# A second level of seven-product multiplication for part of a dense layer, computed among the first sequence products

## The chip, the cores and the metric

The kernel runs on one core of a Trainium2 chip. The metric is the device time of one execution in microseconds (us). About 0.2% of it, 1.7 us, is what a measurement of this kernel can tell from no change.

## The reference

The input is `x` with 2048 tokens of 640 channels. Two branches are computed and mixed by a gate per token.

```python
g = sigmoid((x * gate_w).sum(-1, keepdims=True))
# branch A: Fourier mixing, real part
a = x @ dft_hid_re.T;  b = x @ dft_hid_im.T
A = dft_seq_re @ a - dft_seq_im @ b
# branch B: dense 640 -> 1728, mish, dense 1728 -> 640
h = x @ w1 + b1
B = (h * tanh(softplus(h))) @ w2
return g * A + (1 - g) * B
```

## The kernel before

**Products.** Everything is float32. An operand is kept as a pair of tiles, `h` (rounded to the matmul's format) and `l` (the rest). ACT makes the first (`operand` L328, `split` L319), DVE the second by a subtraction (L329, L320). One block product of 128x128 weights with 128x512 moving data is three matmuls, h·h, h·l and l·h (`mm3`, all on line 334). So every operand that is made costs one row on ACT and one on DVE.

**Seven instead of eight.** Each large product is cut in 2x2 blocks and made by a scheme of seven block products instead of eight, at the price of sums and differences of blocks on DVE (`tt`, L298) and of partial results that are copied out of an accumulator bank and added later. There are eight such banks, `ps0` to `ps7`, of 128x512.

**Stages.** In program order: the sequence products of `x` with the two Fourier matrices (four `Problem`s `sq[0..3]`, each with the phases `first`, `second`, `third`; the results go to DRAM as `u`); the hidden products (`hd`, results `y`); the dense layer with `w1` and mish (`dense_rest`, `dense_first`, results `act`); the last product with `w2` (`ou`), which also adds `y` and writes the output. `gates` computes the gate of every token during the sequence stage.

The first phases of `sq[0]`, `sq[1]` and `sq[2]` open the kernel. In a first phase eight tiles of a Fourier matrix are loaded, made operands and multiplied with three blocks of `x` each: nine matmuls for one new operand.

**The dense layer before.** The outputs are 13 full groups `f` of 128 columns and one of 64. Groups 12 and 13 (`dense_rest`) are made plainly for each of the four token blocks `t` of 512. Groups 0 to 11 are made by `dense_first(tp)`: token blocks 2tp and 2tp+1 are the two rows of blocks, channels 0-255 and 256-511 the two columns, groups `f` and `f+6` the two halves of the weights; channels 512-639 are a plain fifth part (`d1`, `d2`). For each `f` that makes 18 block products: a11 2, s1 2, d2 1, s2 2, s4 2, d1 1, s3 2, a12 2, d1 1, a22 2, d2 1. Two groups `f` go side by side and use all eight banks.

**What sets the order.** The code records each instruction in a `Graph`. PE's order is the order of the code. All other instructions get a due time (`want`, computed backwards from the matmuls that need them in `wants`), and `run` walks through a model of the five engines, hands out buffers (18 tiles `f`, 6 tiles `x`, 10 operand pairs `r`, 26 weight pairs `w`) and writes each engine's instructions in the order in which the model starts them. On the chip each engine then executes its own list strictly in that order. ACT, DVE and the DMA queues therefore run the lists that the model chose, and a row that waits holds up all rows behind it on its engine. SP issues the loads, POOL issues most stores.

Of the kernel before, what the change touches and what calls it, by code (L numbers as in the profile page):

```python
# [47 lines left out]
class Graph:  # L48
# [71 lines left out]

    def run(self, pools):
# [103 lines left out]
def fnet_mish_gate(ctx: ExitStack, tc: tile.TileContext, xn, xt, c_re, c_im, wd_re, wd_im,  # L225
                   w1a, w1b, b1a, b1b, w2, gw, out):
    nc = tc.nc
# [370 lines left out]
    def raw(t, k):  # L598
        return load(FS, xt[t, k])
# [8 lines left out]
    def w1_block(f):  # L608
        if f in W1:
            return  # L610
        ga, gb, t = load(X, w1a[f], cols=D), load(X, w1a[f + FP], cols=D), Val(X)
        a, b, c = W1[f] = Val(W), Val(W), Val(W)
        if f // KD not in T2B:
            T2B[f // KD] = Val(W)
        split(a, 0, ga, 0, D)
        split(b, 2, gb, 2 * P, 3 * P)
        tt(ga, gb, ga, OP.subtract, (A2, A2, A2), n=2 * P)
        tt(t, gb, ga, OP.subtract, (A2, B2, A2), n=2 * P)
# [3 lines left out]
        split(c, 4, t, 0, P)  # L622
        split(T2B[f // KD], f % KD, t, P, P)
        split(b, 0, t, 2 * P, 2 * P)
        split(c, 2, gb, 0, 2 * P)

    def w1_rest():
        if W1C:
            return
        W1C.append(Val(W))  # L630
        split(W1C[0], 0, load(X, w1a[FC - 1], cols=D), 0, D)
# [46 lines left out]

    def dense_first(tp, ready):
        t1, t2 = 2 * tp, 2 * tp + 1  # L680
        x = dict(ready)

        def get(name, make):
            if name not in x:
                x[name] = operand(make(), W if name[0][0] == "a" else R)
            return x[name]

        def sums_of(k):
            if k in summed:
                return  # L690
            summed.add(k)
            a21, a22, a11, a12 = raw(t2, k), raw(t2, k + 2), raw(t1, k), raw(t1, k + 2)
# [4 lines left out]
            raws.update({("s1", k): s1, ("s2", k): a22, ("s3", k): a21, ("s4", k): a12})  # L697
        raws, summed = {}, set()

        def op(name, k=0):  # L700
            if name[0] == "s":
                if (name, k) not in x:
                    sums_of(0)
                    sums_of(1)
                return get((name, k), lambda: raws.pop((name, k)))
            t, kk = {"a11": (t1, 0), "a12": (t1, 2), "a22": (t2, 2), "d1": (t1, 4), "d2": (t2, 4)}[name]
            return get((name, k), lambda: raw(t, kk + k))

        def times(b, name, blocks, start, stop):
            for k, w in enumerate(blocks):  # L710
                mm3(b, w, op(name, k), start and k == 0, stop and k == len(blocks) - 1)

        for f0 in range(0, FP, 2):
            pair_ = (f0, f0 + 1)
            for f in pair_:
                w1_block(f)
            w = {f: W1[f] for f in pair_}
            bk = {f: [bank() for _ in range(4)] for f in pair_}
            p1, p5, u2 = {}, {}, {}
            for f in pair_:  # L720
                times(bk[f][0], "a11", [(w[f][0], k) for k in range(2)], True, True)
                p1[f] = to_sbuf(bk[f][0])
            for f in pair_:
                times(bk[f][1], "s1", [(w[f][2], k) for k in range(2)], True, True)
                p5[f] = to_sbuf(bk[f][1])
            for f in pair_:
                times(bk[f][3], "d2", [(w[f][1], 4)], True, True)
            for f in pair_:
                times(bk[f][0], "s2", [(w[f][2], 4), (T2B[f // KD], f % KD)], False, True)
                u2[f] = to_sbuf(bk[f][0])  # L730
            for f in pair_:
                times(bk[f][1], "s4", [(w[f][1], 2 + k) for k in range(2)], False, False)
                times(bk[f][1], "d1", [(w[f][1], 4)], False, True)
# [5 lines left out]
            for f in pair_:  # L739
# [23 lines left out]

    nc.scalar.preload_act_table_set("sigmoid_and_others")
    ones = nc.const_aps.tensor(1.0, [P, N], mybir.dt.bfloat16)
# [17 lines left out]
    def gates():  # L783
# [8 lines left out]
        cols = [(gcol, k) for k in range(KS)]  # L792
        act(lambda: nc.scalar.activation(gcol.t, gcol.t, AF.Sigmoid), cols, cols, KS)
        dve(lambda: nc.vector.tensor_scalar(qcol.t, gcol.t, -1.0, 1.0, op0=OP.mult, op1=OP.add), cols, whole(qcol), KS)
# [8 lines left out]
    def c_tile(m):  # L803
        return lambda t, k: load(FS, (c_re, c_im)[m][t, k], by=HEAD.get(("c", k), 1e9) if not (m or t) and G.pe < 5 else 1e9)

# [10 lines left out]

    sq = [Problem(seq, q // 2, c_tile(q % 2), put_u(q % 2), aside=aside(f"ps{q}") if q in (1, 2) else None) for q in range(4)]
    hd = [Problem(hid, tp, lambda t, k: load_of(FS, usc[k][t]), put_y, aside=aside("ph") if tp else None,
# [4 lines left out]

    sq[0].first(seq_top)
    sq[1].first(seq_top)
    sq[2].first(seq_top)
    for c, src in ((b1s.t[:, :FC], b1a), (b1s.t[:FR, FC:], b1b)):
        dma("SP", lambda c=c, src=src: nc.sync.dma_start(c, src), [], whole(b1s), P * FC * 4)
    for q in range(4):
        if q == 3:  # L830
            sq[3].first(seq_top)
        sq[q].second(seq.low)
# [5 lines left out]
    for p in hd:  # L838
        p.second(hid.low)
        p.third()  # L840
    for t in (2, 3):
        dense_rest(t, [operand(raw(t, k)) for k in range(KD)])
    have = {}
    for t, names in ((0, ("a11", "a11", "a12", "a12", "d1")), (1, ("a21", "a21", "a22", "a22", "d2"))):
        xs = [operand(raw(t, k), W if n in ("a11", "a12", "a22") else R) for k, n in enumerate(names)]
        for k, n in enumerate(names):
            if n != "a21":
                have[n, k % 2 if k < 4 else 0] = xs[k]
        dense_rest(t, xs)
    dense_first(0, have)  # L850
    dense_first(1, {})
    ou[0].first(fin.top)
# [50 lines left out]
```

## Time and profile before

| | |
|---|---|
| median of three runs | 865.41 us (865.31 to 866.7) |
| the profiled execution's own time | 865.36 us |
| its span, first to last instruction | 863.6 us (1.8 us lie around it) |
| PE busy | 858.6 us, 99% |
| DVE busy | 672.0 us, 78% |
| ACT busy | 460.6 us, 53% |
| moved by DMA | 202.05 MB, mean 234 GB/s |

Nearly the whole span is the chain of matmuls on PE; the other engines have time left over the whole span, but DVE hardly has any in the first 140 us. A busy share over the whole span therefore says little about one stage.

### The profile page before, as it was taken

The page shows a single profiled execution, that of the slowest core. Times are in us where ns is not written, and L with a number is a line of the kernel's source. Part 1 is how long each engine was busy: PE and PEld are TensorE (multiplying, and loading weights), DVE is VectorE, ACT ScalarE, POOL GpSimd, SP SyncE. Part 2 cuts the span into 40 slices and gives each one's busy share as a digit, 9 for nine tenths or more (in the row PEclk, how much of TensorE's full clock was granted, in tenths as well). Part 3 has the DMA queues.
Part 4 walks back from the last instruction along what each step waited for, and adds up shares of the span by engine and source line. Part 5 has one row for each costly group of instructions (what it writes and reads, how often), then busy time and mean ns, then how long its engine had stood idle before and what let it go on. Part 6 is the DMA issues. An engine that isn't in the chain of part 4 may idle for free.

```text
span 863.6 us, 11923 instructions
## 1 busy us (share of the span) xinstructions
PE 858.6 (99%) x3772; PEld 708.0 (82%) x3772; DVE 672.0 (78%) x1183; ACT 460.6 (53%) x829; POOL 78.3 (9%) x142
## 2 busy tenths in 40 slices
PE   9999999999999999999999999999999999999998
PEld 6888888888888888888888888888888888888886
DVE  7999997876786577998878999915677899758493
ACT  7765536544553544777454657745655765533242
POOL 0000002001100200002002002111122100004000
PEclk9999999999999999999999999999999999999999
DMA  9986969764955474759864959455353778638943
GB/s 335 334 275 240 344 227 363 265 214 135 363 170 208 164 256 145 267 184 335 283 198 152 360 196 357 152 188 196 136 172 144 268 287 301 205 117 174 359 167 121
DMA packets 102175, 202.05 MB, mean 234 GB/s; under 512 B 12768, under 2 KB 15584, under 8 KB 102112
## 3 DMA queue, kind: packets, MB, share of 16 engines
q1 hardware_dynamic: 90416, 165.51, 55.8%
q0 software_dynamic: 11552, 35.66, 11.9%
q8 instruction: 29, 0.48, 0.2%
q14 instruction: 34, 0.28, 0.1%
q10 hardware_dynamic: 144, 0.13, 0.0%
HBM read 162.96 MB, written 38.29 MB: 233 GB/s over the span
## 4 chain that ended last, share of the span: by engine, by line
PE 99%; DMA 0%; ACT 0%; DVE 0%; issue 0%; ACTq 0%
PE ps L334 99%; DMA f<-in_xn_dram 0%; ACT f L307 0%; DVE w0l L320 0%; ACT w0h L319 0%; DVE x L580 0%; ACT x L578 0%; DVE r0h L326 0%; ACTq L578 0%; ACTq L307 0%
## 5 line engine op out<-in xcount | busy, mean ns | idle before, releaser
L298 DVE TENSOR_TENSOR f<-f,f 128x512 f32<-128x512 f32 x308 | 207.2, 686 | 14.6 <-DMA f<-in_c_im_dram 5.2
L298 DVE TENSOR_TENSOR f<-ps,f 128x512 f32<-128x512 f32 x99 | 64.8, 685 | 45.7 <-PE ps L334 45.5
L307 ACT ACTIVATE f<-ps 128x512 f32<-128x512 f32 x132 | 76.8, 594 | 38.1 <-PE ps L334 30.3
L290 POOL DMA_DIRECT2D u<-f x40 | 21.5, 540 | 320.7 <-DVE f L298 308.1
L603 ACT ACTIVATE f<-f,b1s 128x512 f32<-128x512 f32 x36 | 25.6, 722 | 29.5 <-DVE f L298 29.3
L290 POOL DMA_DIRECT2D act<-f x52 | 28.2, 542 | 134.7 <-DVE f L298 72.9
L328 ACT ACTIVATE r1h<-f 128x512 fp32r<-128x512 f32 x39 | 24.6, 630 | 28.0 <-PE ps L334 17.8
L328 ACT ACTIVATE r8h<-f 128x512 fp32r<-128x512 f32 x39 | 24.5, 629 | 27.9 <-PE ps L334 17.0
L328 ACT ACTIVATE r2h<-f 128x512 fp32r<-128x512 f32 x38 | 23.9, 630 | 27.1 <-PE ps L334 22.8
L328 ACT ACTIVATE r4h<-f 128x512 fp32r<-128x512 f32 x39 | 24.5, 629 | 25.0 <-PE ps L334 20.7
L328 ACT ACTIVATE r0h<-f 128x512 fp32r<-128x512 f32 x37 | 23.3, 630 | 27.2 <-PE ps L334 16.9
L329 DVE TENSOR_TENSOR r1l<-f,r1h 128x512 fp32r<-128x512 f32 x39 | 26.9, 688 | 12.5 <-ACT r1h L328 12.5
L328 ACT ACTIVATE r6h<-f 128x512 fp32r<-128x512 f32 x38 | 23.9, 628 | 20.9 <-PE ps L334 12.3
L329 DVE TENSOR_TENSOR r5l<-f,r5h 128x512 fp32r<-128x512 f32 x38 | 26.1, 688 | 11.0 <-ACT r5h L328 11.0
L298 DVE TENSOR_TENSOR x<-x,x 128x256 f32<-128x256 f32 (+1 forms) x77 | 32.0, 426 | 3.4 <-DMA x<-in_w_dram 2.0
L329 DVE TENSOR_TENSOR r2l<-f,r2h 128x512 fp32r<-128x512 f32 x38 | 26.1, 688 | 10.8 <-ACT r2h L328 10.8
L328 ACT ACTIVATE r7h<-f 128x512 fp32r<-128x512 f32 x38 | 23.8, 627 | 19.7 <-PE ps L334 16.1
L328 ACT ACTIVATE r3h<-f 128x512 fp32r<-128x512 f32 x38 | 23.9, 629 | 19.3 <-PE ps L334 11.4
L328 ACT ACTIVATE r9h<-f 128x512 fp32r<-128x512 f32 x37 | 23.3, 629 | 19.9 <-PE ps L334 14.2
L329 DVE TENSOR_TENSOR r0l<-f,r0h 128x512 fp32r<-128x512 f32 x38 | 26.2, 689 | 9.5 <-ACT r0h L328 9.2
L328 ACT ACTIVATE r5h<-f 128x512 fp32r<-128x512 f32 x38 | 23.9, 628 | 17.9 <-PE ps L334 15.7
L329 DVE TENSOR_TENSOR r7l<-f,r7h 128x512 fp32r<-128x512 f32 x38 | 26.1, 688 | 9.3 <-ACT r7h L328 9.1
(2005 smaller groups left out, 2661.1 us busy)
## 6 DMA issues: line engine op xcount, KB each, us to landing
f<-in_c_re_dram SPq DMA_DIRECT2D x128, 256.0 KB, 4.6
f<-in_c_im_dram SPq DMA_DIRECT2D x128, 256.0 KB, 4.3
f<-act SPq DMA_DIRECT2D x81, 256.0 KB, 5.1
f<-u SPq DMA_DIRECT2D x80, 256.0 KB, 5.3
act<-f POOLq DMA_DIRECT2D x52, 256.0 KB, 3.0
f<-in_xt_dram SPq DMA_DIRECT2D x44, 256.0 KB, 5.0
u<-f POOLq DMA_DIRECT2D x40, 256.0 KB, 5.5
x<-in_xn_dram SPq DMA_DIRECT2D x24, 320.0 KB, 4.5
```

Source lines behind the costliest of these rows:

```text
L290: dma(queue, lambda: ISSUE[queue].dma_start(d.t, v.t[:rows]), whole(v), whole(d), rows * N * 4)
L298: dve(lambda: nc.vector.tensor_tensor(o.t[rows, x], a.t[rows, y], b.t[rows, z], op=op), whole(a, b), whole(o), n)
L307: act(lambda: nc.scalar.activation(o.t, a.t, AF.Copy, scale=scale), whole(a), whole(o))
L328: act(lambda: nc.scalar.activation(r.t[0][:, :N], src.t[:, :N], AF.Copy), whole(src), [(r, 0)])
L329: dve(lambda: nc.vector.tensor_tensor(r.t[1][:, :N], src.t[:, :N], f32(r.t[0][:, :N]), op=OP.subtract), whole(src) + [(r, 0)], [(r, 1)])
L334: G.add("PE", lambda: nc.tensor.matmul(bank.t, w.t[wn][:, k * P:k * P + P], x.t[xn_][:, :N], start, stop, skip_group_check=True), [(w, (k, ...
L603: act(lambda: nc.scalar.activation(o.t[rows], src.t[rows], AF.Mish, **more), whole(src, table) + whole(b1s) * bias, whole(o), more=0.1)
```

## The change

For token blocks 0 and 1, two of the seven products (a11 with b11, and a12 with b21 together with its fifth part) have to be made for all six `f`. In the changed kernel the pairing of token blocks is (0,2) and (1,3), so that these two products of both pairs, taken over token blocks 0 and 1, over two channel blocks of 128 and over `f` 0-2 against 3-5, are again 2x2 block products. They are made by a second level of seven, in two pieces:

- `early_first` (channels 0-255): 7 block products for each of three units `j`, results stored to DRAM as `early`.
- `early_second` (channels 256-511 and the fifth part): 7 + 4 block products for each unit, added to `early`, then bias, mish and the store to `act`.
- `early_rests`: groups 12 and 13 of token blocks 0 and 1, which were made in the dense stage before.

These pieces stand between the first phases: `sq[1].first`, `early_first`, `sq[2].first`, `early_second`, `sq[3].first`, `early_rests`, `sq[0].first`; then the second and third phases follow. The three units of a piece take turns, one block product (or two) each. `dense_first` now makes 13 block products for each `f`: a11, a12 and one d1 are gone, and the first partial result is loaded from `early`. It uses six banks instead of eight.

Counted over the program, the dense layer has 730 matmuls in place of 748. SP and POOL issue 37 and 15 transfers more, ACT has 66 and DVE 58 instructions more. The mish table is loaded at the start, the sigmoid table for the gates, and the mish table again: three table loads in place of two. `wants` has a new last pass, which moves an instruction's due time behind those of what it needs.

```diff
+        for op in self.ops:
+            if op.engine != "PE":
+                op.want = max([op.want] + [(d.at if d.engine == "PE" else d.want) + d.took for d in op.deps])
...
+    def w1_twice(k0, fifth=False):
+        C, w, at, n, tiles = slice(0, H * P), {}, {}, 0, []
+        for i in range(2):
+            for j in range(2):
+                w[f"b{i + 1}{j + 1}"] = load(FS, w1h[k0 + i, j], cols=H * P)
+        for o, x, y in (("t1", "b12", "b11"), ("t2", "b22", "t1"), ("t3", "b22", "b12"), ("t4", "b21", "t2")):
+            w[o] = Val(FS)
+            tt(w[o], w[x], w[y], OP.subtract, (C, C, C), n=H * P)
...
+    def early_first():
+        at, x = w1_twice(0), x_twice(0)
+        def unit(j):
+            b0, b1, b2 = bank(), bank(), bank()
+            mm3(b0, at["b11", j], x["a11"], True, True)
+            p = to_sbuf(b0)
+            yield
+            mm3(b2, at["t1", j], x["s1"], True, True)
+            yield
+            mm3(b0, at["b21", j], x["a12"], False, True)
+            store(early[0, j], to_sbuf(b0))
+            yield
+            copy(b1, p)
+            mm3(b1, at["t2", j], x["s2"], False, True)
+            u = to_sbuf(b1)
+            yield
+            mm3(b1, at["t3", j], x["s3"], False, True)
+            v = to_sbuf(b1)
+            tt(v, b2, v, OP.add)
+            store(early[1, j + H], v)
+            yield
+            mm3(b1, at["t4", j], x["a22"], False, True)
+            store(early[1, j], to_sbuf(b1))
+            yield
+            mm3(b2, at["b22", j], x["s4"], False, True)
+            tt(u, b2, u, OP.add)
+            store(early[0, j + H], u)
+            yield
+        turns(unit(j) for j in range(H))
...
+        xs = [operand(raw(t2, k), R if k < 2 else W) for k in range(KD)]
+        x.update({("a22", 0): xs[2], ("a22", 1): xs[3], ("d2", 0): xs[4]})
+        dense_rest(t2, xs)
...
             for f in pair_:
-                times(bk[f][0], "s2", [(w[f][2], 4), (T2B[f // KD], f % KD)], False, True)
+                copy(bk[f][0], load_of(FS, early[t1, f]))
+                times(bk[f][0], "s2", [(w[f][1], 4), w[f][3]], False, True)
                 u2[f] = to_sbuf(bk[f][0])
...
             for f in pair_:
-                times(bk[f][0], "s3", [(w[f][2], 2 + k) for k in range(2)], False, True)
+                times(bk[f][0], "s3", [(w[f][1], 2 + k) for k in range(2)], False, True)
+                tt(p5[f], bk[f][2], p5[f], OP.add)
                 tt(p5[f], bk[f][0], p5[f], OP.add)
-            for f in pair_:
-                times(bk[f][2], "a12", [(w[f][0], 2 + k) for k in range(2)], True, False)
-                times(bk[f][2], "d1", [(w[f][0], 4)], False, True)
-                tt(p1[f], bk[f][2], p1[f], OP.add)
-                tt(p5[f], bk[f][3], p5[f], OP.add)
-                out_act(f, t1, p1[f], p1[f])
                 out_act(f + FP, t2, p5[f], p5[f])
             for f in pair_:
-                times(bk[f][0], "a22", [(w[f][1], k) for k in range(2)], False, False)
-                times(bk[f][0], "d2", [(w[f][0], 4)], False, True)
+                times(bk[f][0], "a22", [(w[f][0], k) for k in range(2)], False, False)
+                times(bk[f][0], "d2", [w[f][2]], False, True)
...
-    sq[0].first(seq_top)
     sq[1].first(seq_top)
-    sq[2].first(seq_top)
...
+    early_first()
+    sq[2].first(seq_top)
+    early_second()
+    sq[3].first(seq_top)
+    early_rests()
+    sq[0].first(seq_top)
```

**Place 1: PE, 110 matmuls after the start.** `ps` are banks, `r` and `w` operands. Before, PE was here in the first phase of `sq[1]`, which adds into three banks and reads none of them until its end:

```order
L334 MATMUL ps3_68<-r2h_77,w4l_126 128x512
L334 MATMUL ps4_69<-r2h_77,w4h_125 128x512
L334 MATMUL ps4_69<-r2l_78,w4h_125 128x512
L334 MATMUL ps4_69<-r2h_77,w4l_126 128x512
L334 MATMUL ps5_70<-r2h_77,w4h_125 128x512
L334 MATMUL ps5_70<-r2l_78,w4h_125 128x512
L334 MATMUL ps5_70<-r2h_77,w4l_126 128x512
L334 MATMUL ps3_68<-r3h_79,w5h_127 128x512
```

Now PE is here in `early_first`, from the end of the t2 product of the first unit to the start of its t3 product:

```order
L337 MATMUL ps0_65<-r9h_91,w13l_144 128x512
L337 MATMUL ps2_67<-r9h_91,w13h_143 128x512
L337 MATMUL ps2_67<-r9l_92,w13h_143 128x512
L337 MATMUL ps2_67<-r9h_91,w13l_144 128x512
L337 MATMUL ps3_68<-r9h_91,w13h_143 128x512
L337 MATMUL ps3_68<-r9l_92,w13h_143 128x512
L337 MATMUL ps3_68<-r9h_91,w13l_144 128x512
L337 MATMUL ps0_65<-w11h_139,w14h_145 128x512
```

Bank `ps0` has to be copied out by ACT between the first row and the last, that is within seven rows; before, no copy stood there.

**Place 2: ACT, first operands of the dense stage.** `r` and `w` written from `f` are token operands, `w` written from `x` are pieces of weights. Before, the token operands stood behind each other in front of the first dense matmul:

```order
L319 ACTIVATE w21h_159<-x5_116 128x256
L328 ACTIVATE r7h_87<-f10_103 128x512
L328 ACTIVATE r9h_91<-f5_98 128x512
L328 ACTIVATE r0h_73<-f14_107 128x512
L328 ACTIVATE r2h_77<-f4_97 128x512
L328 ACTIVATE r1h_75<-f1_94 128x512
```

Now the last two token operands, `w17` and `w12`, stand behind pieces of weights:

```order
L322 ACTIVATE w20h_157<-x2_113 128x384
L322 ACTIVATE w1h_119<-x4_115 128x384
L322 ACTIVATE w15h_147<-x5_116 128x256
L331 ACTIVATE w17h_151<-f13_106 128x512
L322 ACTIVATE w23h_163<-x1_112 128x256
L331 ACTIVATE w12h_141<-f12_105 128x512
```

The row `w15h` reads `x5`, which DVE has to make first; `w17h`, for which PE waits, comes behind it. On DVE the rows there are now these, from a read of the bank `ps4` at the end of the hidden products to the second part of the operand `w17`:

```order
L301 TENSOR_TENSOR f9_102<-ps4_69,f16_109 128x512
L323 TENSOR_TENSOR w24l_166<-x1_112,w24h_165 128x128
L301 TENSOR_TENSOR x5_116<-x2_113,x5_116 128x256
L301 TENSOR_TENSOR x1_112<-x4_115,x1_112 128x256
L323 TENSOR_TENSOR w22l_162<-x3_114,w22h_161 128x256
L323 TENSOR_TENSOR w15l_148<-x5_116,w15h_147 128x256
L301 TENSOR_TENSOR x0_111<-x2_113,x5_116 128x256
L332 TENSOR_TENSOR w17l_152<-f13_106,w17h_151 128x512
```

PE has nine matmuls between its last row into `ps4` and the first row with `w17h`, and one more before the row with `w17l`.

**Place 3: ACT, in the middle of `early_second`.** Before, at about as many matmuls, ACT had operands of the sequence stage and one copy out of a bank behind a piece of weights, `w18h`, which waits for DVE:

```order
L319 ACTIVATE w11h_139<-x2_113 128x128
L328 ACTIVATE r1h_75<-f9_102 128x512
L328 ACTIVATE r2h_77<-f6_99 128x512
L319 ACTIVATE w18h_153<-x4_115 128x512
L307 ACTIVATE f16_109<-ps6_71 128x512
```

Now the copies out of banks for the units are mixed with operands of the coming `sq[3].first`:

```order
L331 ACTIVATE r4h_81<-f14_107 128x512
L310 ACTIVATE f9_102<-ps7_72 128x512
L310 ACTIVATE f2_95<-ps1_66 128x512
L331 ACTIVATE r5h_83<-f10_103 128x512
L331 ACTIVATE r6h_85<-f0_93 128x512
L310 ACTIVATE f14_107<-ps4_69 128x512
L310 ACTIVATE f1_94<-ps7_72 128x512
```

The copy `f14<-ps4` stands behind `r5h` and `r6h`, which need tiles of a Fourier matrix from DRAM.

More of the change, by code (lines that the diff above doesn't have):

```diff
@@ L677, in dense_rest @@
         out_act(FC, t, a, a, FR, False)
[L679 to L686, printed above, removed]
+    H = FP // 2
+    early = {(t, f): dram(f"early{t}_{f}") for t in range(2) for f in range(FP)}
+    def w1_twice(k0, fifth=False):
[6 more added lines that the diff above has]
+            tt(w[o], w[x], w[y], OP.subtract, (C, C, C), n=H * P)
+        if fifth:
+            for j in range(2):
+                w["d", j] = load(FS, w1h[KD - 1, j], cols=H * P)
+        for o in ("b11", "b21", "t2", "t1", "t3", "t4", "b22") + (("d", 0), ("d", 1)) * fifth:
+            i = 0
+            while i < H:
+                if n % KD == 0:
+                    tiles.append(Val(W))
+                m = min(H - i, KD - n % KD)
+                split(tiles[-1], n % KD, w[o], i * P, m * P)
+                for e in range(m):
+                    at[o, i + e] = tiles[-1], n % KD + e
+                i, n = i + m, n + m
+        return at
@@ new lines, in x_twice @@
+    def x_twice(k0):
+        a11, a12, a21, a22 = (raw(t, k) for t in (0, 1) for k in (k0, k0 + 1))
+        x = {"a11": operand(a11, W), "a12": operand(a12, W), "a22": operand(a22, W)}
+        if k0:
+            x["a21"] = operand(a21, W)
+        s1 = fresh(FS, a21, a22, OP.add)
+        tt(a21, a11, a21, OP.subtract)
+        tt(a11, s1, a11, OP.subtract)
+        tt(a12, a12, a11, OP.subtract)
+        x.update(s1=operand(s1), s2=operand(a11), s3=operand(a21), s4=operand(a12))
+        return x
@@ L688, in sums_of, with early_rests, dense_first @@
+    kept = {}
+    def early_rests():
+        for t, ks in ((0, ("a11", "a12")), (1, ("a21", "a22"))):
+            dense_rest(t, [operand(raw(t, k)) for k in range(2)] + [kept[k] for k in ks] + [kept["d"][t]])
+    def dense_first(tp):
+        t1, t2 = tp, tp + 2
+        x, raws = {}, {}
         def sums_of(k):
-            if k in summed:
-                return
-            summed.add(k)
             a21, a22, a11, a12 = raw(t2, k), raw(t2, k + 2), raw(t1, k), raw(t1, k + 2)
@@ L803, in c_tile @@
     def c_tile(m):
[L804 removed]
+        return lambda t, k: load(FS, (c_re, c_im)[m][t, k], by=HEAD.get(("c", k), 1e9) if G.pe < 5 else 1e9)
     def put_u(m):
@@ L840, in fnet_mish_gate @@
         p.third()
[L841 to L851, printed above, removed]
+    w1_rest(True)
+    dense_first(0)
+    dense_first(1)
     ou[0].first(fin.top)
```

109 lines of the change are left out of this document (79 added, 30 removed).

## The prediction

> **What bounds the kernel now.** I read the page's first part, then the chain of work that ended last in order of time (start, us, what), then groups, windows and short stretches of the timeline.
>
> ```profile
> PE 858.6 (99%) x3772; PEld 708.0 (82%) x3772; DVE 672.0 (78%) x1183; ACT 460.6 (53%) x829; POOL 78.3 (9%) x142
> ...
> 0.74 2.25 DMA f<-in_xn_dram
> ...
> 4.65 50.22 PE ps L334 x215
> ...
> 55.33 0.59 ACT f L307
> 55.91 0.04 issue
> 55.96 803.89 PE ps L334 x3545
> 859.85 0.02 issue
> 859.87 0.02 ACTq L578
> 859.88 0.04 issue
> 859.93 0.39 ACT x L578
> ```
>
> The chain is PE from 4.65 to 859.85 us, broken once. A matmul costs 803.89 / 3545 = 0.2268 us, so the time can only change through the number of matmuls or through gaps on PE. The timeline shows the one gap:
>
> ```profile
> 54.79 0.63 ACT L319 ACTIVATE w18h<-x 128x512 fp32r<-128x512 f32 x1 [1.07 <-DVE x L298]
> ...
> 55.33 1.06 ACT L307 ACTIVATE f<-ps 128x512 f32<-128x512 f32 x2
> 55.37 0.39 PE L334 MATMUL ps<-r4h,w0l 128*128 128x512 f32 x1
> ...
> 55.96 0.50 PE L334 MATMUL ps<-r4h,w0h 128*128 128x512 f32 x1 [0.20 <-ACT f L307]
> ...
> 56.29 0.40 PE L334 MATMUL ps<-r4l,w0h 128*128 128x512 f32 x1
> ```
>
> From 55.37 to 56.29 two matmuls started in 0.92 us instead of 0.45: 0.47 us lost. The copy out of the bank stood behind the piece of weights `w18h`, and that waited for DVE. This is the pattern to look for in the changed lists.
>
> **The change part by part.** The sum is made against the profiled execution, 865.36 us, 0.05 us under the median.
>
> *Matmuls removed.* 730 instead of 748: 18 x 0.2268 = 4.08 us less.
>
> *The gap at 55 us.* The `w18h` row no longer stands before that copy: 0 to 0.47 us less. I take 0.45; new gaps have terms of their own.
>
> *The added work on DVE and ACT* lies almost all in the first 100 us. Are they full there? The windows (span; PE, PEld, DVE, ACT, POOL; clock, DMA share, GB/s):
>
> ```profile
> 44.00:93.00 49.00, 48.80 (x215) 40.07 (x215) 46.97 (x97) 31.26 (x60) 1.61 (x3) 1.00 0.79 275
> ```
>
> DVE was full (46.97 of 49.00 us), yet PE hardly waited: DVE made weights ahead. So I add up DVE's list up to the row that the 500th matmul (4.65 + 500 x 0.2268 = 118 us) needs. What a row costs is the time to the next row's start:
>
> ```profile
> 62.37 0.28 DVE L320 TENSOR_TENSOR w21l<-x,w21h 128x128 fp32r<-128x128 f32 x1
> 62.57 0.68 DVE L320 TENSOR_TENSOR w20l<-x,w20h 128x512 fp32r<-128x512 f32 x1
> 63.17 0.69 DVE L329 TENSOR_TENSOR r6l<-f,r6h 128x512 fp32r<-128x512 f32 x1
> 63.78 0.42 DVE L298 TENSOR_TENSOR x<-x,x 128x256 f32<-128x256 f32 x1
> 64.11 0.69 DVE L329 TENSOR_TENSOR r7l<-f,r7h 128x512 fp32r<-128x512 f32 x1
> ```
>
> That is 0.20, 0.60 and 0.33 us for 128, 512 and 256 columns. By these DVE had 96 us of rows due by then and has 88 us now, because the weights of the second phases are due later. The added rows cost nothing behind this cover; without it, 0.60 us for each 512-column row too many. ACT has a third table load:
>
> ```profile
> L798 ACT ACT_TABLE_LOAD x1 | 1.3, 1283 | 0.0
> ```
>
> It stands in the first phase of `sq[0]`, whose operands lie tens of matmuls ahead: 0, or at most its 1.28 us if that lead were gone. The added 13 MB of DMA are the first rival below. The start (same first rows) and the end are unchanged: 0, with 0.3 us either way.
>
> *Short waits in `early_first` (place 1).* What a bank needs between its last matmul and the next one into it:
>
> ```profile
> L334 PE MATMUL ps<-r3h,w1h 128*128 128x512 f32 x17 | 6.6, 389 | 0.0
> ...
> L307 ACT ACTIVATE f<-ps 128x512 f32<-128x512 f32 x132 | 76.8, 594 | 38.1 <-PE ps L334 30.3 <-DMA u<-f 2.0 <-issue 1.6
> ...
> L298 DVE TENSOR_TENSOR f<-ps,f 128x512 f32<-128x512 f32 x99 | 64.8, 685 | 45.7 <-PE ps L334 45.5
> ```
>
> The matmul runs 0.39 us; 0.08 us pass until the reader starts (859.85 to 859.93 in the chain), the copy takes 0.59, and 0.04 us later PE goes on (55.91): 1.10 us, with a DVE read 1.20 us. Seven rows from start to start give 7 x 0.2268 = 1.59 us. So ACT may come 0.49 us late. In the two rounds of t2 to t4 it has six copies, 0.53 us each (55.33: two in 1.06), and one operand between them, 0.54 us:
>
> ```profile
> 60.34 0.63 ACT L319 ACTIVATE w20h<-x 128x512 fp32r<-128x512 f32 x1 [0.58 <-DVE x L298]
> 60.88 0.62 ACT L328 ACTIVATE r5h<-f 128x512 fp32r<-128x512 f32 x1
> ```
>
> Together 6 x 0.53 + 0.54 = 3.7 us, beside 18 matmuls, 4.1 us. Each copy waits for its bank in turn, so the operand makes one copy about 0.1 to 0.2 us late. Before that ACT takes three banks of `sq[1]` and six of the first rounds in a row, another 0.1 us late. I take 0.3 us; the bounds are 0 and 2 us (an ACT row held up by a load, as at 54.79, where the idle time was 1.07, once or twice). *`early_second`* has two such waits of seven rows and a load in front of a copy: 0.2 us, 0 to 1.5.
>
> *Start of the dense stage (place 2).* Count from the start of PE's last row into `ps4`. It ends and DVE begins 0.47 us later; its rows `f9` 0.60 and `w24l` 0.20 pass, `x5` runs 0.42; then ACT's `w15h` passes in 0.32 and `w17h` runs 0.63, with 0.04 between engines twice: 2.72 us. The rows for 256 columns on ACT:
>
> ```profile
> 65.17 0.42 ACT L319 ACTIVATE w6h<-x 128x256 fp32r<-128x256 f32 x1 [0.73 <-DVE x L298]
> 65.49 0.29 ACT L319 ACTIVATE w23h<-x 128x128 fp32r<-128x128 f32 x1
> ```
>
> PE wants `w17h` 10 x 0.2268 = 2.27 us after that start, so it waits 0.45 us. `w17l` comes after five more rows of 0.33 us from 1.27 us on, at 2.92, and is done at 3.61 + 0.04; PE wants it at 2.49: 1.16 us in all. DVE has read banks without pause before that, so it may reach `f9` up to 1.3 us late. I take 1.3 us, bounds 0.5 and 2.5.
>
> *Banks in `dense_first`.* Between s3 and a22 the block a12 is gone: the next matmul into a bank that DVE has to read stands 7 rows later (once for each `f` pair) or 10 rows later, where it was 25. For 7 rows 1.59 - 1.20 = 0.39 us are free. A 512-column row that DVE has just begun costs up to 0.60, so at worst 0.21 us are lost where one row is in the way. Twelve places: 0 to 2.5 us (12 x 0.21); most rows in front are short, so I take 0.5.
>
> The sum: -4.08 - 0.45 + 0.3 + 0.2 + 1.3 + 0.5 = -2.23, so 865.36 - 2.23 = 863.1 us.
>
> **The rivals.** *Transfers of the first 62 us (slower).* In place 3 the copy `f14<-ps4` stands behind `r5h` and `r6h`, which need tiles from DRAM. PE wants that bank at matmul 258, 63.2 us, so the tile of `r6h` has to land by 61.9 us. Ahead of it I count 69 loads and 19 stores, 21.6 MB. The first tile landed at 3.0 us (0.74 + 2.25); after that this means 21.6 / 58.9 = 367 GB/s, the point from which it decides. What was moved before:
>
> ```profile
> 0.00:66.00 66.00, 64.72 (x271) 51.05 (x272) 58.88 (x118) 46.36 (x92) 3.62 (x10) 1.00 0.91 316
> 9.00:30.00 21.00, 21.00 (x95) 17.38 (x94) 19.36 (x35) 17.62 (x35) 0.00 (x0) 1.00 1.05 389
> ```
>
> At 389 GB/s, the rate of the stretch that is full, the tile lands at 58.5 us; at 316 from the start on at 68.4 us, 6.5 us late, and 863.1 + 6.5 = 869.6 us. The second rate holds pauses in which SP waited for buffers; new stores in front of loads speak for more of these. I give it 0.13, with prices from 2 to 6.5 us. The Trainium skill, DMA: Bandwidth & Descriptors, Specifications, puts a core's limit to HBM at about 358 GB/s; by that the tile would land 1.4 us late (21.6 / 0.358 = 60.3, plus 3.0), an estimate of 864.5 us. The row with 389 GB/s disagrees with it, and the measurement decides. The Trainium skill, TensorE: Matmul & The Clock Gate, Part 1, says that PE's clock halves after an idle window of about 3.4 us; a gap as long as this rival's would then cost some 2 us more. Only the gap at 55.37 is in the trace, and the second matmul behind it took 0.40 us, so no run here shows this.
>
> *Every short wait is late.* If one 512-column row stands in front at all 22 short places (10 on ACT in the early pieces, 12 on DVE), 22 x 0.21 = 4.6 us come in place of the 1.0 us above: 863.1 + 3.6 = 866.7 us. For it: both engines are busy there. Against: most rows in front are short, and the model spaced them. 0.13.
>
> *Nothing waits but the dense start at its lower bound:* 865.36 - 4.08 - 0.47 + 0.5 = 861.3 us. 0.14. That the removal does nothing can't be: the matmuls are gone from PE's list.
>
> **How the numbers follow.** My forecast has 0.60, its own range is 861.5 to 865.0. 0.2% of the time, 1.7 us, is about what a measurement of this kernel can tell from no change; faster means under 863.7, slower over 867.1. Faster: 0.14 from the last rival and 0.39 of the forecast's 0.60, 0.53. Same: 0.20 of the forecast and 0.07 of the late waits, 0.27. Slower: 0.13 + 0.06 + 0.01, 0.20. The range leaves out the long end of the transfers and the lowest corner: 861.2 to 867.0.
>
> **What would show it.** PE has 3754 matmuls and the same interval. A gap of 1 to 1.5 us stands where the dense stage starts, released by ACT `w17h` and DVE `w17l`. Between 27 and 35 us there are a few tenths, released by copies out of banks. DVE stays full to 175 us without a PE gap. I would be wrong if the waits of PE name a DMA or an operand in the first 75 us, or if they add up to more than 3 us.

## The result

| | runs | median us | profiled execution | matmuls |
|---|---|---|---|---|
| before | 4 | 865.57 (865.31 to 866.70) | 865.36 us, span 863.6 | 3772 |
| after | 4 | 873.60 (873.34 to 874.41) | 874.41 us, span 872.3 | 3754 |

The change made the kernel slower by 8.0 us. The ratio is 1.0092, 95% interval 1.0074 to 1.0109. The page of the profile after, its first part and the row of the granted clock:

```profile
PE 859.0 (98%) x3754; PEld 705.2 (81%) x3754; DVE 697.2 (80%) x1241; ACT 485.9 (56%) x896; POOL 86.5 (10%) x157
...
PEclk9998999999999999999999999999999999999999
```

The 18 matmuls are gone, and yet PE is "busy" for 0.4 us more than before; one slice of the clock is below 9. The waits of PE (the line it waited for; us in total, times, longest):

```profile
PE ps L337 <- ACT f L310: 4.4, 4, 3.2
PE ps L337 <- ACT w17h L331: 1.5, 1, 1.5
PE ps L337 <- ACT r1h L331: 1.0, 1, 1.0
...
PE ps L337 <- DVE w17l L332: 0.5, 1, 0.5
PE ps L337 <- DVE f L301: 0.4, 1, 0.4
```

Before, behind the start, there was one such gap, of 0.47 us. The longest one now stands in `early_second`. PE's timeline there (start us, us, what, in brackets the idle time before it and what ended it):

```profile
66.30 0.40 PE L337 MATMUL ps<-r2h,w13l 128*128 128x512 f32 x1
69.90 0.80 PE L337 MATMUL ps<-r2h,w13h 128*128 128x512 f32 x1 [3.21 <-ACT f L310]
70.50 0.63 PE L337 MATMUL ps<-r2l,w13h 128*128 128x512 f32 x1
70.92 0.63 PE L337 MATMUL ps<-r2h,w13l 128*128 128x512 f32 x1
71.35 0.63 PE L337 MATMUL ps<-w18h,w9h 128*128 128x512 f32 x1
```

Two losses are seen. From 66.30 to 69.90 nothing starts. Behind that the starts are 0.43 us apart where 0.227 is usual: 13 intervals, until 76 us. The windows give the clock of this stretch (span; PE, PEld, DVE, ACT, POOL; clock, DMA share, GB/s):

```profile
0.00:62.00 62.00, 59.28 (x249) 46.12 (x250) 52.34 (x102) 50.41 (x103) 10.61 (x23) 1.00 0.94 326
...
70.00:75.00 5.00, 5.00 (x12) 3.94 (x13) 3.48 (x8) 2.07 (x5) 0.00 (x0) 0.50 1.05 403
```

ACT's timeline shows what the copy waited for, SP's when the two loads were issued, and the chain of waits why the second one was not issued sooner:

```profile
67.25 0.63 ACT L331 ACTIVATE r5h<-f 128x512 fp32r<-128x512 f32 x1 [1.78 <-DMA f<-in_c_im_dram]
68.73 0.63 ACT L331 ACTIVATE r6h<-f 128x512 fp32r<-128x512 f32 x1 [0.86 <-DMA f<-in_c_im_dram]
69.27 1.55 ACT L310 ACTIVATE f<-ps 128x512 f32<-128x512 f32 x3
```

```profile
61.17 0.95 SPq L283 DMA_DIRECT2D f<-in_c_im_dram  x2
```

```profile
55.47 6.31 DMA ps<-f
61.78 0.02 issue
61.80 6.92 DMA f<-in_c_im_dram
...
69.27 0.59 ACT f L310
69.86 0.04 issue
69.90 2.50 PE ps L337 x5
```

The two loads are issued at 61.17 and 61.80 us and take about 6.1 and 6.9 us; ACT waits 1.78 us for the tile of `r5h` and 0.86 us more for that of `r6h`. The buffer for the tile of `r6h` held a partial sum that had first to be stored (6.31 us); only then could its load be issued. On SP's list the load for `r5h` stands behind another one (`f<-early`) that waited 1.3 us for the first of the same stores. `r6h` stands on ACT ahead of three copies out of banks, and the bank of the first is what PE waits for. The landing times between 45 and 72 us, first of before, then of after (KB each, median us from issue to landing):

```profile
f<-in_c_re_dram SPq DMA_DIRECT2D x16, 256.0 KB, 4.6
...
ps<-f POOLq DMA_DIRECT2D x3, 256.0 KB, 4.1
```

```profile
f<-in_c_im_dram SPq DMA_DIRECT2D x8, 256.0 KB, 6.5
...
ps<-f POOLq DMA_DIRECT2D x3, 256.0 KB, 6.3
```

At the start of the dense stage the picture is the one of the prediction's place 2, but larger. The rows are PE's last into `ps4`, DVE's (the second of the two at 578.36 is `f9`), then ACT's and PE's:

```profile
577.24 0.39 PE L337 MATMUL ps<-r7h,w21l 128*128 128x512 f32 x1
```

```profile
578.36 1.28 DVE L301 TENSOR_TENSOR f<-ps,f 128x512 f32<-128x512 f32 x2
579.56 0.28 DVE L323 TENSOR_TENSOR w24l<-x,w24h 128x128 fp32r<-128x128 f32 x1
```

```profile
580.20 0.42 ACT L322 ACTIVATE w15h<-x 128x256 fp32r<-128x256 f32 x1 [6.09 <-DVE x L301]
580.52 0.61 ACT L331 ACTIVATE w17h<-f 128x512 fp32r<-128x512 f32 x1
```

```profile
581.19 0.50 PE L337 MATMUL ps<-w17h,w25h 128*128 128x512 f32 x1 [1.52 <-ACT w17h L331]
582.17 0.50 PE L337 MATMUL ps<-w17l,w25h 128*128 128x512 f32 x1 [0.48 <-DVE w17l L332]
```

### The profile page after: what moved, and what is told of

It is laid out like the page before. It is cut to its first block, busy times and chain, and to the rows that moved or that the text cites. A ratio compares the mean times of both kernels' runs of the same rounds, so it can differ in the third digit from the quotient of the medians.

```text
span 872.3 us, 12120 instructions
## 1 busy us (share of the span) xinstructions
PE 859.0 (98%) x3754; PEld 705.2 (81%) x3754; DVE 697.2 (80%) x1241; ACT 485.9 (56%) x896; POOL 86.5 (10%) x157
## 4 chain that ended last, share of the span: by engine, by line
PE 87%; DVE 6%; DMA 4%; issue 1%; ACT 1%; SPq 0%; POOL 0%; ACTq 0%; DVEq 0%
PE ps L337 87%; DVE f L301 2%; DMA f<-in_c_im_dram 1%; DMA x<-in_w_dram 1%; DMA f<-in_xt_dram 1%; DMA ps<-f 1%; DVE x L301 1%; DMA f<-early 0%; ACT f L310 0%; DVE r1l L332 0%; DVE w13l L323 0%; SPq L283 0%; DVE w16l L323 0%; DVE r5l L332 0%; DVE w19l L323 0%
## 5 line engine op out<-in xcount | busy, mean ns | idle before, releaser
L301 DVE TENSOR_TENSOR f<-f,f 128x512 f32<-128x512 f32 (+2 forms) x327 | 218.1, 681 | 12.1 <-ACT f L606 4.2
L310 ACT ACTIVATE f<-ps 128x512 f32<-128x512 f32 x138 | 79.4, 595 | 24.6 <-PE ps L337 20.1
L301 DVE TENSOR_TENSOR f<-ps,f 128x512 f32<-128x512 f32 x108 | 70.8, 683 | 23.7 <-PE ps L337 17.0
L293 POOL DMA_DIRECT2D u<-f x40 | 21.6, 542 | 320.0 <-DVE f L301 309.3
L332 DVE TENSOR_TENSOR r3l<-f,r3h 128x512 fp32r<-128x512 f32 x38 | 26.1, 687 | 11.0 <-ACT r3h L331 10.8
L310 ACT ACTIVATE ps<-f 128x512 f32<-128x512 f32 x57 | 33.5, 595 | 1.9 <-DVE f L301 1.7
```

The source lines that it names most:

```text
L293: dma(queue, lambda: ISSUE[queue].dma_start(d.t, v.t[:rows]), whole(v), whole(d), rows * N * 4)
L301: dve(lambda: nc.vector.tensor_tensor(o.t[rows, x], a.t[rows, y], b.t[rows, z], op=op), whole(a, b), whole(o), n)
L310: act(lambda: nc.scalar.activation(o.t, a.t, AF.Copy, scale=scale), whole(a), whole(o))
L332: dve(lambda: nc.vector.tensor_tensor(r.t[1][:, :N], src.t[:, :N], f32(r.t[0][:, :N]), op=OP.subtract), whole(src) + [(r, 0)], [(r, 1)])
```

## The experiments

My theory after the result: the first 75 us hold more DMA than fits, loads land 5 to 8 us after their issue, and the lists, which the planner orders by 2.2 us and 370 GB/s, put rows that wait for such loads ahead of copies that PE needs. The rival: the early products leave ACT and DVE too little time wherever they stand, whatever the DMA does.

To read the runs side by side I add up, in the matmuls' starts of one profiled execution of each, what an interval is over 0.2268 us where that is more than 0.05 us, by place. e1 to e12 and e14 ran once each, with the kernel before on the same chip at 865.67 to 866.02 us; e13's time is a median, its profiled execution took 864.78 us. The changed kernel itself took 873.34 to 874.41 us in its four runs, so the times of e1, e4 and e5 can't be told from it.

| run | start | 55-76 us | 468-486 us | 576-620 us | other places | time us |
|---|---|---|---|---|---|---|
| before | 1.27 | 0.47 | 0 | 0 | 0 | 865.36 |
| after | 1.90 | 7.49 | 0.85 | 2.64 | 1.05 | 874.41 |
| e1 | 2.04 | 2.04 | 4.83 | 2.31 | 2.05 | 873.39 |
| e2 | 2.35 | 6.79 | 6.36 | 4.18 | 3.92 | 883.85 |
| e3 | 1.69 | 0.43 | 0 | 1.23 | 5.74 | 871.26 |
| e4 | 1.42 | 1.13 | 0 | 1.82 | 9.10 | 873.74 |
| e5 | 2.26 | 2.56 | 4.77 | 2.45 | 0.97 | 873.42 |
| e6 | 1.60 | 4.10 | 2.93 | 2.11 | 1.26 | 872.62 |
| e7 | 1.65 | 3.23 | 1.87 | 2.53 | 1.69 | 871.45 |
| e8 | 1.61 | 8.77 | 0 | 5.32 | 1.71 | 878.16 |
| e9 | 1.71 | 3.33 | 2.29 | 2.44 | 1.39 | 871.38 |
| e10 | 1.13 | 3.61 | 0 | 2.52 | 0.67 | 868.86 |
| e11 | 1.59 | 0.24 | 4.92 | 2.92 | 1.75 | 872.95 |
| e12 | 1.67 | 2.43 | 0 | 1.73 | 0.11 | 866.61 |
| e13 | 2.29 | 0.47 | 0 | 1.50 | 0.11 | 864.51 |
| e14 | 4.24 | 2.81 | 4.69 | 2.30 | 2.34 | 876.64 |

**e1: without the stored partial sums of `sq[2]`.**

```diff
-            if self.aside:
+            if self.aside and self is not sq[2]:
                 for d, v in zip(self.aside, self.p1 + [self.d]):
                     store(d, v)
...
-                self.p1 = [load_of(FS, d) for d in self.aside[:2]]
-                self.d = load_of(FS, self.aside[2])
+                left = [usc[j][0] for j in range(3)] if self is sq[2] else self.aside
+                self.p1 = [load_of(FS, d) for d in left[:2]]
+                self.d = load_of(FS, left[2])
```

> Left out: the three stores of sq[2]'s first partial results and their reading back (other stored tiles are read in their place). Turnaround theory (the 3.6 us gap at 66 us comes from one buffer that has to be stored before the tile of r6h can be loaded into it, and from a copy that stands behind r6h on ACT): the gap goes, the clock stays at 1.0, about 874.4 - 7 = 867.5 us. Bytes theory (only the amount of data moved by then counts): 0.8 MB less is 2.1 us at 370 GB/s, so a gap of about 1.5 us stays, the clock stays at 1.0, about 869.5 us.

873.39 us. At 66 us only 0.72 us were lost and no half clock followed, so these three stores made most of that wait. Whether by the buffers' turn or by their bytes (0.8 MB less) is not shown, and the lists differ from 17 us on. The time did not follow: 4.83 us came at 470 us, where 0.85 had stood.

**e2: the gates' loads later.**

```diff
-            x = load(X, tokens[k], cols=D)
+            x = load(X, tokens[k], usc[0][0], cols=D)
```

> The loads of the gates' tokens wait for the first stored result of the sequence stage, so two to four of them (0.33 MB each) no longer stand ahead of the tiles of r5h and r6h. Bytes theory: 0.7 to 1.3 MB less, 1.8 to 3.5 us earlier, the gap at 66 us under 2 us, the clock at 1.0, about 869 us. Turnaround theory: the store of that buffer and the load into it are still there and only less crowded; the gap keeps more than 2 us, 870 to 874 us.

883.85 us, a miss for both. The edit orders all lists anew, and the new ones wait in other places too (1.62 us at 130). It tells nothing about the bytes.

**e3: `dense_rest` of tiles 0 and 1 back at the dense stage.**

```diff
-    early_rests()
     sq[0].first(seq_top)
...
     w1_rest(True)
+    for t in (0, 1):
+        dense_rest(t, [operand(raw(t, k)) for k in range(KD)])
     dense_first(0)
```

> Groups 12 and 13 of token blocks 0 and 1 are made at the start of the dense stage again (50 matmuls, 11.3 us, with operands of their own). Theory of the lost cover (between the hidden products and dense_first there are 25 matmuls instead of 100, so DVE has the last y rows and the first weights at the same time): the gap of 2.4 us at 579 us goes. Rival (the operands in weight tiles stand behind weights in any case): it stays. The gaps of the first 80 us stay much as they are; about 872 us by the first, 874 by the rival.

871.26 us. The dense start lost 0.80 us in place of 2.55: that fits that the rests (25 matmuls for each token block, 50 here) had been the cover in which DVE catches up, and that the change took them away. But all lists are new, and at 17 to 39 us they lost over 4 us.

**e4: all early pieces at the start of the dense stage.**

```diff
-    early_first()
     sq[2].first(seq_top)
-    early_second()
     sq[3].first(seq_top)
-    early_rests()
     sq[0].first(seq_top)
...
+    early_first()
+    early_second()
+    early_rests()
     w1_rest(True)
     dense_first(0)
```

> All three early pieces stand at the start of the dense stage, the four first phases follow each other at the start. Theory that the place is what costs: the gap at 66 us and the half clock go (7.1 us), what stays is 4.1 us of matmuls removed and the waits in the pieces and at the dense stage, 3 to 4 us: 864 to 866 us. Rival (the pieces are short of cover anywhere): waits of more than 6 us in the pieces, 868 us and more.

873.74 us. 55 to 76 us lost 1.13, but the pieces lost 5.88 us at 530 to 539 us, half clock included. The pieces are short of cover in either place; this speaks for the rival, since the first 75 us are relieved here.

**e5, e6, e7: rows moved by hand.** The lists and the buffers are those of the changed kernel; the planned rows of an engine are only issued in another order. In e5 on ACT (and `r5l`, `r6l` on DVE behind the additions that follow):

```diff
-L331 ACTIVATE r5h<-f_103 128x512
-L331 ACTIVATE r6h<-f_93 128x512
 L310 ACTIVATE f_107<-ps_69 128x512
 L310 ACTIVATE f_94<-ps_72 128x512
 L310 ACTIVATE f_110<-ps_66 128x512
 L310 ACTIVATE f_96<-ps_69 128x512
+L331 ACTIVATE r5h<-f_103 128x512
+L331 ACTIVATE r6h<-f_93 128x512
```

> The changed kernel with two rows of ACT's list (r5h<-f, r6h<-f, and DVE's r5l, r6l) put behind the four copies f<-ps of early_second that they stood ahead of; every other row of every engine keeps its place, buffers and DMAs too. If those two rows, which wait for a DMA, cause the wait at 66 us: the gap there (3.4 us) goes, the 13 slow matmuls after it (2.9 us) run at 0.227 us, and the time is 874.4 - 6.5 = about 867.9. If the DMA itself is short there (the rival: too many bytes for the rate), PE waits for r5h or r6h some 60 matmuls later instead and the time stays above 872.

In e6 on ACT (and `w17l`, `w12l` on DVE ahead of `w24l`, `x5`, `x1`, `w22l`, `w15l`):

```diff
+L331 ACTIVATE w17h<-f_106 128x512
+L331 ACTIVATE w12h<-f_105 128x512
 L322 ACTIVATE w15h<-x_116 128x256
-L331 ACTIVATE w17h<-f_106 128x512
 L322 ACTIVATE w23h<-x_112 128x256
-L331 ACTIVATE w12h<-f_105 128x512
```

> The changed kernel with the dense stage's first tiles sooner: ACT's w17h and w12h ahead of w15h, DVE's w17l and w12l ahead of the five rows on x and w that they stood behind; nothing else moves. If the order on ACT and DVE makes the wait at 579 us: of 2.55 us some 1.5 to 2.3 go, 874.4 - 1.9 = about 872.5. If the tile's DMA lands late there, nothing changes: 874.4.

> Both moves of rows together. If the two waits are independent and are what the change lost: 874.4 - 6.5 - 1.9 = about 866.0, within 1 us of the kernel before. If later stages give it back: above 868.

873.42, 872.62 and 871.45 us. Each move does its work at its place: 1.31 us instead of 6.95 at 64 to 76 us in e5, 0.40 instead of 2.55 at 578 us in e6. Neither gives its price. In e6 the next wait, 1.40 us at 586 us, took most of the gain back. And e6 has the lists of the changed kernel up to 569 us, e9 below has them up to 447 us, yet at 55 to 76 us they lost 4.10 and 3.33 where the changed kernel lost 7.49: after 64 us it is 2.45 and 2.54 instead of 6.95, without half clock, and ACT waits 1.50 and 1.33 us for the tile of `r5h` and not for that of `r6h`. So the length of the wait changes from run to run, and 6.95 is one execution's. At 471 us e6 lost 2.93 where the changed kernel lost 0.85: what is lost early is not lost again there. e5, with little lost early, lost 4.77 there. The whole is steadier than its places.

**e8, e9, e10: the planner's landing time, and more cover at the dense start.**

```diff
-DELAY, RATE = 2.2, 370e3
+DELAY, RATE = 4.5, 370e3
```

> The changed kernel with one constant of the planner set by what the trace shows: DELAY, the time from a DMA's issue to its landing that the lists are ordered by (beside the bytes at RATE), 4.5 us instead of 2.2; all lists are ordered anew, matmuls and DMAs stay the same. If rows that wait for a DMA ahead of bank copies on ACT are the main loss (they stand there because the planner takes their tiles as landed), the waits of PE for ACT's f rows at 64-76 and 470-476 us shrink to under 1 us each without half clock: 867 to 870. If the early products simply leave DVE and ACT too little time (the rival), the waits move and the sum stays: 872 to 875.

```diff
...
-        dense_rest(t2, xs)
+        if not tp:
+            dense_rest(t2, xs)
+            dense_rest(3, [operand(raw(3, k)) for k in range(KD)])
```

> The changed kernel with the last 64 features of both later token tiles (dense_rest for tiles 2 and 3) made at the start of the dense stage, 30 matmuls (6.8 us) instead of 15 between the sequence products and the first product of seven. If the dense start waits because DVE's list is behind and the cover of 15 matmuls is short: the 2.55 us at 579 us fall to under 1 us and the waits of 0.3 to 1.4 us up to 600 us do not come: 872 to 873. If DVE stays behind as far, the same wait comes some 15 matmuls later: 874 to 875.

> Both rests first, and DELAY 3.5 us. If the two losses add: 866 to 869; if waits only move: 871 to 875.

878.16, 871.38 and 868.86 us. A longer landing alone was a miss: the wait at 470 us went, those at 55 to 76 us grew to 8.77 with half clock. With both rests first and 3.5 us it is the best so far. I had no reason for 3.5 beside 4.5, and these runs don't give one. In e9 the wait for `w17` is gone (the cover is 50 matmuls in place of 25 in the trace, not 30 in place of 15), but the next wait, for a copy into a bank, comes at 589 us, and the place lost 2.44 us in all where the changed kernel lost 2.64. So e9's 871.38 us, 2 us under the changed kernel, can't be put down to that place, and why e10 has 868.86 us stays open.

**e11: the same lists, fewer bytes.** Each load of the first phases from 17 to 95 us moves a quarter of its columns; the planner still counts the whole. GpSimd fills the tiles once at the start, which delays the first matmul by 1.2 us.

```diff
-        v = Val(pool)
-        op = dma(queue, lambda: ISSUE[queue].dma_start(v.t[:rows, :cols], src() if callable(src) else src),
+        v, c = Val(pool), cols // 4 if 17 < G.pe < 95 and (callable(src) or len(src.shape) == 2) else cols
+        op = dma(queue, lambda: ISSUE[queue].dma_start(v.t[:rows, :c], (src() if callable(src) else src)[:, :c] if c < cols else src() if callable(src) else src),
...
```

> The changed kernel with its lists as they are, but every load that belongs to the first phases between 17 and 95 us (tiles of c_re, c_im, xt, w1h, w1a, the tokens for the gates and the stored early sums) moves only the first quarter of its columns; the rest of each tile keeps what it held, so the sums are not the reference's. If the transfers set the waits of 55 to 76 us (DMA was at a share of 0.97 to 1.05 there): they go, 0.54 + 6.95 us, and no half clock comes there: 866 to 868. If the order of the lists alone sets them, whatever the DMA does, a gap of over 2 us stays at 66 us: 872 to 875.

The windows, and the chain of waits from 40 to 62 us:

```profile
40.00:62.00 22.00, 22.00 (x99) 18.23 (x98) 21.70 (x45) 18.50 (x41) 3.14 (x6) 1.00 0.62 195
62.00:76.00 14.00, 14.00 (x62) 11.24 (x61) 12.77 (x26) 11.65 (x22) 2.70 (x6) 1.00 0.84 282
```

```profile
39.92 22.21 PE ps L337 x98
```

From 9 to 468 us PE loses 0.24 us in all, with every row of every list where the changed kernel has it (GpSimd's fills aside). This decides between the theories for the first 76 us: in these lists the transfers set those waits, not the work of ACT and DVE; the 1.2 us by which PE starts later are less than the wait of 3.4 us. Farther on the rival keeps its part: in e4 the pieces wait at 530 us, and the dense start waits for DVE's list. The time, 872.95 us, missed the expected 866 to 868, because the late start cost 1.2 us and the wait at 468 us came in full. The chain ahead of that one (start us, us, what):

```profile
450.32 8.06 DMA x<-in_w1a_dram
458.40 0.42 DVE x L301
...
469.13 0.60 DVE r5l L332
...
471.24 0.59 ACT f L310
471.87 2.54 PE ps L337 x8
```

Blocks of weights for the dense stage are made here; their 320 KB load took 8.06 us, and then ACT's row `w8h`, ahead of a copy, waited for DVE's list. In this chain there is no PE row between 427 and 471 us; in the chain of the changed kernel PE stands up to 464.54 us. This fits a preparation with a pace of its own, for which a PE that comes late waits less; no run changes this place alone, so that stays an argument.

**e12, e13, e14: lists that fit.**

```diff
-DELAY, RATE = 2.2, 370e3
+DELAY, RATE = 4.5, 390e3
...
-        dense_rest(t2, xs)
+        if not tp:
+            dense_rest(t2, xs)
+            dense_rest(3, [operand(raw(3, k)) for k in range(KD)])
...
-    sq = [Problem(seq, q // 2, c_tile(q % 2), put_u(q % 2), aside=aside(f"ps{q}") if q else None) for q in range(4)]
+    sq = [Problem(seq, q // 2, c_tile(q % 2), put_u(q % 2), aside=aside(f"ps{q}")) for q in range(4)]
...
-    sq[1].first(seq_top)
+    sq[0].first(seq_top)
...
     early_rests()
-    sq[0].first(seq_top)
+    sq[1].first(seq_top)
```

> The changed kernel with three edits: the first phase of sq[0] first and that of sq[1] last (now the two change places), both rests first at the dense stage, and the planner's DELAY 4.5 us and RATE 390 GB/s, near what the traces show. If the waits come from lists that take loads as landed too soon, lists made with the real landing keep rows that wait for a DMA behind the copies, and the waits fall from 14 us to 6 to 8: 865 to 867. If the early work is simply too much for its place: 869 or more, as in the run with both rests first and 3.5 us.

The first results of `sq[0]`, which now comes first, are stored and read back too. 866.61 us, as expected. One long wait of the known kind is left; ACT's timeline:

```profile
68.36 0.63 ACT L331 ACTIVATE r5h<-f 128x512 fp32r<-128x512 f32 x1 [1.77 <-DMA f<-in_c_im_dram]
68.90 1.07 ACT L310 ACTIVATE f<-ps 128x512 f32<-128x512 f32 x2
```

e13 puts that one row behind the two copies, by hand (and `r5l` on DVE behind three additions):

```diff
-L331 ACTIVATE r5h<-f_95 128x512
 L310 ACTIVATE f_97<-ps_67 128x512
 L310 ACTIVATE f_94<-ps_69 128x512
+L331 ACTIVATE r5h<-f_95 128x512
```

> The kernel of the run before (c_re's first phase first, both rests first, DELAY 4.5 and RATE 390) with one operand of the sequence stage, r5h on ACT and r5l on DVE, put behind the two copies f<-ps on ACT and the four additions on DVE that they stood ahead of. If that row alone makes the wait at 67 us (2.43 us, ACT waited 1.77 us for its load): 866.6 - 2.4 = 864.2, below the kernel before. If the wait moves on to a later row: 865.5 to 867.

864.51 us, the median of 12 runs, against 865.89 us of before on the same chip: ratio 0.998, interval 0.9971 to 0.9988. It is 9 us faster than the changed kernel and 1.4 us under the kernel before; the interval excludes 1, but 1.4 us is less than the 1.7 us that a measurement of this kernel is taken to tell. The stretch from 62 us on, and the copy's row:

```profile
62.00:76.00 14.00, 13.80 (x61) 11.09 (x60) 13.26 (x26) 10.87 (x20) 2.71 (x5) 1.00 1.02 387
```

```profile
67.52 1.07 ACT L310 ACTIVATE f<-ps 128x512 f32<-128x512 f32 x2
69.20 0.64 ACT L331 ACTIVATE r5h<-f 128x512 fp32r<-128x512 f32 x1 [0.61 <-DMA f<-in_c_im_dram]
```

The load is as late as it was (DMA share 1.02), but now only `r5h` waits for it, whose matmuls come 48 rows later. e13 loses 4.38 us in all, before 1.74: 865.36 - 4.08 + 2.64 = 863.92 us, and its profiled execution took 864.78. The 0.9 us between them are not in the sum; in the changed kernel it is as much (865.36 - 4.08 + 12.19 = 873.47 for 874.41).

The phases changed round, without the other edits:

> The changed kernel with only the first phases of sq[0] and sq[1] changed round; DELAY 2.2 us and the rests as in the changed kernel. If the landing time that the planner assumes makes most of the gain of the two runs before: 870 to 873 here, with waits over 2 us at 470 and 579 us. If the order of the phases makes it: 866 to 868.

876.64 us: not better than the changed kernel. Of its loss 4.24 us lie at the start, where PE ran with starts 0.43 us apart up to 12.4 us; the changed kernel loses 1.90 there, and without the difference it would be 874.3 us. So the order of the phases doesn't make the gain by itself, and e8 showed that the landing time doesn't either. Which of the edits of e12 does how much stays open; they were tried together, and each new plan moves everything. The new last pass of `wants`, which also orders the lists anew, is in every run; what it alone costs or gains is not shown.

## Why the prediction was wrong

The forecast was 863.1 us, faster; the time lies 6.6 us above the range. Its terms against the trace after:

| term | predicted us | measured us |
|---|---|---|
| 18 matmuls | -4.08 | -4.08 |
| gap at 55 us | -0.45 | +0.07 (0.54 for 0.47) |
| start | 0 | +0.7 (1.90 for 1.27, first matmul 0.10 later) |
| `early_first` | +0.3 | 0 |
| `early_second` | +0.2 (0 to 1.5) | 6.95 |
| dense start | +1.3 (0.5 to 2.5) | 2.55 |
| banks in `dense_first` | +0.5 (0 to 2.5) | 1.14 |
| 475 us | none | 0.85 |

These give 8.2 us; the matmuls' starts end 8.56 us later, and the profiled time is 9.05 us longer, the rest being intervals too short to count and 0.35 us outside the span.

*The step that failed is the term of `early_second` and the chance of the transfers.* Place 3 was the right row: the copy `f14<-ps4` behind `r5h` and `r6h`. I put the tile's landing at 58.5 us by 389 GB/s, the rate of a stretch full of loads that wait for nothing, and gave the case in which it does not hold 0.13. The row for 0 to 62 us has 326 GB/s, below the rival's 367, and the tile landed at 68.71 us. I counted bytes and a rate, and not the turn of a buffer, store and then load, at the landing times of a full DMA. SP's list waited 1.3 us for one such store ahead of the load for `r5h` and 0.2 us for another ahead of that for `r6h`, so the two loads were issued at 61.17 and 61.80 us, and then took 6.1 and 6.9 us. For the buffer of `r6h` store and load are 13.2 us. e11 shows that the transfers make the wait in these lists, and e13, in another plan, that 2 us hang on a single row ahead of a copy.

That the rival's numbers come near (68.4 us, 6.5 us) is in part luck. By 326 GB/s its 21.6 MB are through at 66.3 us. And it wants the bank at 4.65 + 258 x 0.2268 = 63.2 us, which leaves out what PE loses at the start: before, the 258th matmul starts at 64.72 us, after at 66.30. So PE's long wait was 3.4 us and not 6.5; the half clock (3.0 us with the slow start behind the gap) and a smaller wait at 64 us (0.6) make up the 6.95.

That term right, the forecast would still have failed. e1, e5 and e11 lost 0.2 to 2.6 us at 55 to 76 us, but 4.8 to 4.9 us at 470 us, and took 872.95 to 873.42 us. The preparation of the dense stage's weights there is a term that I put at nothing: I walked through the three places and `dense_first` alone. In the profiled execution after it shows as 0.85 us only, which fits a PE that came late; why it costs what it does stays open.

*The half clock.* I called some 2 us for it unproved. It came: 13 intervals at 0.43 us, 2.6 us. Starts 0.43 us apart had been in the trace before too, three at 5.2 to 6.5 us, at the start.

*The dense start* was the right mechanism and 1.25 us too small. I let DVE reach `f9` up to 1.3 us late. It came 1.25 us late, at 578.96 us, 1.72 us after the start of PE's last row into `ps4` where the walk has 0.47; it had been busy without pause from 560 us on. With that delay the walk gives 1.16 + 1.25 = 2.41 us, near the 2.55. So the walk held, and I had put almost none of the delay into the 1.3 us that I took. e3 points to what I missed: the rests that the change moves away seem to have been the cover there. The wait that I named as the kind to look for, a copy behind a piece of weights that waits for DVE, also came at 475 us, outside the stages that I walked through.

*Right:* the matmuls and their interval, `early_first` with its banks free in seven rows, the banks in `dense_first` within their bounds, DVE without a gap at 100 to 175 us. Of the two marks of being wrong that I had named one came true: behind the start the first 75 us have 3.8 us of waits. The other did not as I worded it: PE's waits there name copies, and the load stands behind the copy.

## What to carry to other kernels

Where lists are fixed ahead, a load's landing has to be taken from the stretch in which it will run, and the turn of its buffer (the store that empties it, then the load) counted at that pace; a row that waits for a load doesn't belong ahead of a copy that frees a bank within a few matmuls. Here work moved into a stretch where DMA is at a share near 1 met late loads there, and work moved out of a place seems to have taken its cover away. A place that loses little may do so only because PE comes late to it. A change that saves matmuls can be judged only with a plan that fits it: here the same 18 matmuls gave +8 us with one plan and -1.4 us with another.

## What was not expected of the hardware

The clock gave way after shorter gaps than I had thought. A gap is here what an interval between starts has over 0.2268 us. Behind the start, in all 16 profiles, no gap of up to 1.96 us that stands alone was followed by starts 0.43 us apart; of ten from 2.07 to 2.82 us three were (4 to 7 intervals), two of these with another gap of 0.75 or 2.13 us within 5 us; all seven from 2.94 to 3.41 us were (6 to 13). The Trainium skill, TensorE: Matmul & The Clock Gate, Part 1, puts it at an idle window of about 3.4 us and says that the window runs freely; that a gap of 2.51 us has an effect (e2 at 56 us) and one of 2.82 us none (e6 at 471 us) agrees with the second, the shorter gaps don't with the first. So a gap of about 3 us costs 4.7 to 6.4 us here (e14 at 473 us, after at 66 us).

One core moved 403 GB/s from 70 to 75 us, at a share of 1.05. The Trainium skill, DMA: Bandwidth & Descriptors, Specifications, has about 358 GB/s, half of what two cores share; the trace of a kernel on one core lies above it here too.
